# A gated long convolution on one core: fourth stage and projections in two column halves, sums and differences two tiles ahead, late taps in two pieces

## The chip, the cores and the metric

The kernel runs on one core of a Trainium2 chip. The metric is the device time of one execution in microseconds (us). The kernel before took 1112.37 us, the median of three runs that lie between 1107.36 and 1112.41 us. The profile is of one execution of its own, which took 1113.34 us; the span in the profile, from the first to the last instruction, is 1111.3 us.

In this text PE is the matrix engine and PEld its weight loads, DVE the vector engine, ACT the scalar engine, POOL the GpSimd engine, and SP the engine that issues the DMAs.

## The reference, cut to what matters

```python
def _attn_ref(x, h):                     # x: 8 x 6400 x 128, h: 6400 x 128, float32
    B, S, D = x.shape
    Xf, Hf = np.fft.rfft(x, n=2 * S, axis=1), np.fft.rfft(h, n=2 * S, axis=0)
    return np.fft.irfft(Xf * Hf[None], n=2 * S, axis=1)[:, :S, :]

def _moe_ref(x, w_val, conv_w, w_out):   # w_*: 128 x 128, conv_w: 5 x 128
    xp = np.concatenate([np.zeros((B, 4, D)), x], axis=1)
    gate_pre = sum(conv_w[k] * xp[:, k:k + S, :] for k in range(5))
    gate = 1.0 / (1.0 + np.exp(-gate_pre))
    return gate * (x @ w_val) @ w_out    # x is what _attn_ref returned
```

A causal convolution over 6400 steps for each of 128 channels and 8 batches, then a gate from five taps of its result, a projection, the product of both, and a second projection. All of it is float32.

## The kernel before, in words

**The transform.** The convolution is done by a real transform of length 6400 = 100 x 64, in stages that are matrix products. A time step t is 64 * n1 + n2. *Stage one* (`Forward`) folds the first 50 values of n1 onto the last 50: it needs the sum and the difference of two halves of a tile of x, and multiplies each with a constant `r1_sb`. *Stage two* (`s2_mm`) transforms over the 64 values of n2 with the matrices `m2`, of which four blocks are held at a time; `Product` multiplies its result with the spectrum of h (`h_sb`, kept in DRAM as `hd`). *Stage three* (`s3_quads`) is the inverse over 64, and *stage four* (`Chunk.s4`) the inverse over 100, with constants `m4_sb`. Stage four leaves channels on the partitions, and chunks of five n2 with 100 times each; `CHUNKS` has twelve of them and a first one of four (`HEAD`).

**Each chunk** then goes through `copies` (ACT: start the tap sums, copy the chunk `y`, scale one tap into `p`), `taps` (DVE: three multiply-adds of 500 columns; POOL: the fourth tap from `p`), `project` (PE: with `w_val`), `sigm` (ACT), `gate` (DVE), `output` (PE: with `w_out`) and `store` (ACT copy, then a DMA).

**The order** is written by hand and kept (`_Engines`, lines 88 to 105): each engine's queue runs in the order of the program text, so a wait of its front instruction holds all behind it. All instructions are recorded on line 96, which is that helper's; groups are told apart by the tiles they write and read (`pt` is any PSUM tile, `m_sb` stands for `m4_sb` and for the parts of it that hold input tiles in the startup, `r_sb` for both constants).

- *Startup*: stage one for h and for x of batch 0 (16 halves of a tile each; an input tile `x_sb` holds 8 channels of both halves and serves two calls of `half`), then stage two of both in turn, `Spectrum` and `Product`, for 13 blocks `kb`.
- *For each batch b*, stage three in 16 steps g, and beside it, half by half, stage one of the next batch (lines 570 to 584). `sums`, every second g, gives POOL the difference into `d_sb` and DVE the sum in place into the x tile; the matrix products of that tile come right behind, in the same step. The last chunks of the batch before are finished beside it, one item of `trail` a step. In batch 0, which has no such items, the loads of `m4_sb` and 22 small DVE operations that decode the weights (`weights`, one `next` each) stand there instead.
- Then stage four in 13 steps s, and beside it stage two of the next batch with its products (lines 592 to 625). A step gives PE: stage two of block s + 1, `project` of chunk s - 2, stage four of chunk s, `output` of chunk s - 3. It gives DVE: `mul_u` (named `gy<-pt,h` in the profile) and `mul_t` (`w<-pt,h`) of block s, with `taps` of chunk s - 1 between them, then `gate` of chunk s - 2. POOL adds the product terms (`gy<-gy,w`).
- Chunks from `DEFER` on (50 and 55) are *late*: only `y` is copied in stage four, and their taps (four on DVE, read from SBUF), gate and store are items of `trail`.

PSUM has two tiles of two banks for stages one and two and four single banks for the rest (in the startup four tiles of two banks).

Of the kernel before, what the change touches and what calls it, by code (L numbers as in the profile page):

```python
# [15 lines left out]
C = 128  # L16
# [8 lines left out]
XG = 8  # L25
NS = C // (2 * XG)
NQ = 2 * NS
NW = 2 * C + TAPS
CH = 5
# [5 lines left out]
DEFER = 50  # L35
# [3 lines left out]
XB = 2  # L39
# [69 lines left out]
def longconv_moe(ctx: ExitStack, tc: tile.TileContext, x, h, r1, m2, r3, m4, w64, out):  # L109
# [24 lines left out]
    d_sb = [cp.tile([128, XG, N2], F32, name=f"d_{i}") for i in range(2)]  # L134
# [74 lines left out]
    class Forward:  # L209


        def __init__(self, src, dst, xs=x_sb):
            self.src, self.dst, self.xs, self.n, self.i = src, dst, xs, 0, 0
# [7 lines left out]
        def sums(self):  # L221
            j = self.i // 2
            x, d = self.xs[j % len(self.xs)], d_sb[j % 2]
            nc.gpsimd.tensor_tensor(out=d, in0=x[:, 0], in1=x[:, 1], op=ALU.subtract)
            nc.vector.tensor_tensor(out=x[:, 0], in0=x[:, 0], in1=x[:, 1], op=ADD)

        def half(self):
            j, q = self.i // 2, self.i % 2
            self.i += 1
            x, d = self.xs[j % len(self.xs)], d_sb[j % 2]  # L230
            pt = pair()
            for m in range(4):
# [9 lines left out]
            if q:  # L242
                self.load()
            v = pt[:, :, : 4 * N1].rearrange("p r (d t k) -> p r d k t", t=2, k=N1)
            d0 = 4 * j + 2 * q
            return [
                lambda e, r=r: e(self.dst[:, r * C // 4 + d0 : r * C // 4 + d0 + 2], v[:, r]) for r in range(2)
            ]
# [109 lines left out]
    class Chunk:  # L358
# [8 lines left out]
        def s4(self):  # L367
            a, n = self.ch
            pt = single()
            for q in range(n):  # L370
                for c in range(2):
                    nc.tensor.matmul(
                        pt[:, q * N1 : (q + 1) * N1],
                        lhsT=dv[:, a + q, c, :],
                        rhs=m4v(a + q, c),
                        start=c == 0,
                        stop=c == 1,
                    )
            self.p = pt[:, : n * N1].rearrange("p (n t) -> p n t", n=n)
# [34 lines left out]
        def taps(self):  # L414
            a, n = self.ch
            if self.late:
                self.init()
# [8 lines left out]
            if k < n:  # L426
# [10 lines left out]
        def project(self):  # L437
# [3 lines left out]
            nc.tensor.matmul(self.v, lhsT=w_sb[:, :C], rhs=self.y, start=True, stop=True)  # L441
# [9 lines left out]
        def output(self):  # L451
# [3 lines left out]
            for i, o in cells(*self.ch):  # L455
                nc.tensor.matmul(self.o[:, i : i + o.shape[1]], lhsT=w_sb[:, C : 2 * C], rhs=o, start=True, stop=True)
# [13 lines left out]
        for i in range(6)  # L470
    ]
    fh, fx = Forward(h, gh, xh), Forward(x[0], gy, xh)
    nc.sync.dma_start(r1_sb, r1)
    fh.load(NS)
    for f in (fh, fx):
        for g in range(NQ):
            if g % 2 == 0:
                f.sums()
            e = f.half()
            if f is fh and g % 2:  # L480
                fx.load()
            e[0](act)
            e[1](act if g % 2 else dve)
        if f is fh:
            next(wgen)
# [4 lines left out]
    for kb in range(-1, NKB + 1):  # L490
# [8 lines left out]
        if 0 <= kb < NKB:  # L499
            pr[kb].mul_u()  # L500
# [6 lines left out]
    class Gates:  # L507
# [5 lines left out]
        def trail(self):  # L513

            h, i, j, k = (self.cs[i] for i in (0, NCH - 3, NCH - 2, NCH - 1))
            before = self.cs[NCH - 4]
# [20 lines left out]
        def each(self, what, s, last=True):  # L537
            c = self.at(s, last)
            if c:
# [10 lines left out]

    def m4_load(a, k):
        k = N2 + 1 if k == N2 else k
        nc.sync.dma_start(m4_sb[:, a:k], m4.rearrange("k (n t) -> k n t", t=N1)[:, a:k])
# [5 lines left out]
    for b in range(B):  # L559
# [26 lines left out]
        for _ in wgen:  # L586
            pass
# [86 lines left out]
```

## Time and profile before

| what | us |
|---|---|
| median of three runs | 1112.37 |
| the profiled execution | 1113.34 |
| its span | 1111.3 |
| startup, stage one of h and x (8.3 to 63.2) | 54.9 |
| startup, stage two of both (63.2 to 120.7) | 57.5 |
| stage three of batch 0, with stage one of batch 1 | 59.3 |
| stage three of batches 1 to 6, with stage one of the next, mean | 53.2 |
| stage four of batches 0 to 6, with stage two of the next, each | 73.3 |
| stage three of batch 7, nothing beside it | 39.7 |
| stage four of batch 7, nothing beside it, to the end | 59.1 |

The stages were told apart by the first matrix product of each kind: the stages three of batches 0 to 7 begin at 120.7, 253.3, 379.8, 507.0, 632.6, 758.8, 886.2 and 1012.5 us, the stages four at 180.0, 306.5, 433.7, 559.2, 685.4, 812.9, 939.2 and 1052.3 us. A float32 product is two instructions of the profile (two passes), each with its weight load. In a row of the timeline, the first number is the start and the second the length in us; the ends of pipelined matrix products are modelled, so the pace of a run of them is read from one start to the next.

### The profile page before, as it was taken

The numbers are of one execution on the slowest core, as the hardware profiler recorded it, in microseconds if no ns is written. First come the engines' busy times: TensorE is split into PE (matmuls) and PEld (weight loads), VectorE is DVE, ScalarE is ACT, GpSimd is POOL, SyncE is SP. The second block draws the span as 40 slices with busy tenths as digits, with TensorE's granted clock in tenths as the row PEclk, the third lists the DMA queues.
The fourth block names the chain that finished last, engine by engine and source line by source line (L and its number), as shares of the span: only waits on it lengthen the run. The fifth ranks groups of instructions, "written<-read, shape, count | busy, mean of one in ns | idle before, by whom it ended". The sixth has DMA issues, their size and how long they took to land.

```text
span 1111.3 us, 48967 instructions
## 1 busy us (share of the span) xinstructions
PE 1037.6 (93%) x22480; PEld 880.6 (79%) x22480; DVE 757.9 (68%) x1070; ACT 441.2 (40%) x825; POOL 447.1 (40%) x388
## 2 busy tenths in 40 slices
PE   6898779999999999999999999998999999999997
PEld 5798678877887778877898778877798778876875
DVE  2345656886588766987578765987578765986375
ACT  3332232543334443344434433343334443344365
POOL 3335412662156511753246511763136611753022
PEclk9999999999999999999999999999999999999999
DMA  6447634746266542756356552766346452751012
GB/s 246 153 142 234 253 126 144 229 135 223 84 193 187 186 149 89 234 158 216 96 176 187 163 181 86 226 162 231 96 151 198 128 212 69 240 157 50 20 34 85
DMA packets 86909, 175.80 MB, mean 158 GB/s; under 512 B 42288, under 2 KB 50736, under 8 KB 86704
## 3 DMA queue, kind: packets, MB, share of 16 engines
q1 hardware_dynamic: 86704, 172.68, 49.4%
q8 instruction: 176, 2.88, 1.1%
q14 instruction: 29, 0.24, 0.1%
HBM read 139.88 MB, written 32.77 MB: 155 GB/s over the span
## 4 chain that ended last, share of the span: by engine, by line
PE 86%; DVE 4%; issue 4%; DMA 2%; ACT 2%; POOL 1%; POOLq 0%; SPq 0%; DVEq 0%; ACTq 0%
PE pt L96 86%; DVE gl L96 2%; DMA x<-xl 2%; DVE dt L96 1%; DVE x L96 1%; POOL d L96 1%; ACT dt L96 1%; ACT gl L96 0%; DMA x<-hl 0%; ACT yl L96 0%; ACT gy L96 0%; POOL gy L96 0%; POOL dt L96 0%; DVE gy L96 0%; POOLq L670 0%
## 5 line engine op out<-in xcount | busy, mean ns | idle before, releaser
L96 PE MATMUL pt<-r_sb,gy 64*64 64x128 f32 (+1 forms) x8192 | 268.8, 273 | 26.2 <-issue 20.2
L96 PEld LDWEIGHTS pt<-r_sb,gy 64*64 64x64 f32 (+1 forms) x8192 | 236.6, 130 | 67.1 <-issue 40.0
L96 POOL TENSOR_TENSOR gy<-gy,w 128x512 f32<-128x512 f32 (+1 forms) x206 | 250.9, 1243 | 75.5 <-DVE w L96 74.7
L96 PEld LDWEIGHTS pt<-m_sb,dt 128*128 128x128 f32 x2048 | 242.8, 192 | 42.9 <-issue 35.8
L96 ACT COPY dt<-pt 128x512 f32<-128x512 f32 (+3 forms) x270 | 157.0, 585 | 248.2 <-PE pt L96 238.4
L96 PE MATMUL pt<-m_sb,dt 128*128 128x100 f32 x2048 | 244.9, 275 | 3.7 <-DVE dt L96 3.7
L96 PEld LDWEIGHTS pt<-gy,m 128*64 128x64 f32 x6400 | 197.1, 136 | 37.7 <-PE pt L96 28.9
L96 PE MATMUL pt<-gy,m 128*64 128x64 f32 x6400 | 209.4, 222 | 2.2 <-PE pt L96 2.1
L96 POOL TENSOR_TENSOR d<-x 128x512 f32<-128x512 f32 x60 | 76.4, 1279 | 273.4 <-DMA x<-xl 165.9
L96 DVE COPY dt<-pt 128x512 f32<-128x512 f32 (+1 forms) x136 | 92.9, 683 | 106.1 <-PE pt L96 87.1
L96 DVE SCALAR_TENSOR_TENSOR dt<-pt,w_sb,dt 128x500 f32<-128x500 f32 (+7 forms) x216 | 132.9, 631 | 39.5 <-ACT p L96 21.6
L96 PE MATMUL pt<-r_sb,d 50*64 50x100 f32 x2304 | 153.3, 277 | 1.3 <-issue 1.3
L96 PE MATMUL pt<-r_sb,x 50*64 50x100 f32 x1920 | 118.8, 258 | 23.3 <-DVE x L96 14.8
L96 PEld LDWEIGHTS pt<-r_sb,d 50*64 50x64 f32 x2304 | 132.9, 154 | 3.4 <-issue 3.4
L96 DVE COPY gy<-pt 128x400 f32<-128x400 f32 x120 | 68.9, 574 | 88.9 <-ACT gy L96 88.9
L96 DVE TENSOR_TENSOR gy<-pt,h 128x1024 f32<-128x1024 f32 (+1 forms) x98 | 115.0, 1173 | 19.3 <-PE pt L96 19.3
L96 PEld LDWEIGHTS pt<-r_sb,x 50*64 50x64 f32 x1920 | 102.7, 140 | 32.0 <-DVE x L96 18.7
L96 ACT ACTIVATE dt<-pt,w_sb 128x500 f32<-128x500 f32 (+1 forms) x64 | 40.0, 626 | 202.2 <-PE pt L96 202.2
L96 PE MATMUL pt<-dt,w_sb 128*128 128x500 f32 (+2 forms) x240 | 118.4, 583 | 0.4 <-ACT dt L96 0.4
L96 DVE TENSOR_TENSOR w<-pt,h 128x1024 f32<-128x1024 f32 (+1 forms) x98 | 114.8, 1171 | 0.0
L96 POOL TENSOR_TENSOR dt<-dt,p 128x500 f32<-128x500 f32 (+1 forms) x64 | 66.2, 1034 | 110.0 <-DVE dt L96 101.4
L96 DVE SCALAR_TENSOR_TENSOR gl<-pt,w_sb,gl 128x500 f32<-128x500 f32 (+3 forms) x119 | 74.1, 623 | 47.2 <-ACT gl L96 21.8
(38 smaller groups left out, 831.0 us busy)
## 6 DMA issues: line engine op xcount, KB each, us to landing
m<-m SPq DMA_DIRECT2D x96, 512.0 KB, 5.0
h<-hd SPq DMA_DIRECT2D x84, 512.0 KB, 4.8
x<-xl SPq DMA_DIRECT2D x58, 512.0 KB, 3.8
out<-dt SPq DMA_DIRECT2D x56, 250.0 KB, 4.1
out<-yl SPq DMA_DIRECT2D x40, 250.0 KB, 2.5
m_sb<-hl SPq DMA_DIRECT2D x6, 512.0 KB, 7.6
m_sb<-xl SPq DMA_DIRECT2D x6, 512.0 KB, 3.5
hd<-h SPq DMA_DIRECT2D x6, 512.0 KB, 5.4
```

The costliest lines, as they stand in the source:

```text
L96: return self._tc.keep_in_program_order(call(*args, **kwargs))
```

## The change

Seven edits, in the order of the diff:

1. A tile of x has 4 channels instead of 8 (`XG`), and one call of `half` uses it up; three input tiles instead of two, and three tiles `sd_sb` that hold sum and difference, instead of sums in place and two `d_sb`.
2. `sums` is called two tiles ahead of `half`. In the loop over batches both operations go to POOL; in the startup the sum stays on DVE. The next input load is issued by `sums`.
3. Stage four, `project` and `output` give PE two products of 64 columns of the weights where there was one of 128, into the two halves of the PSUM partitions.
4. Both results of stage one are taken out of PSUM by ACT in the loop over batches (before: one by ACT, one by DVE).
5. Chunk 45 becomes late too (`DEFER`), and the taps of the late chunks are issued in two pieces of two taps, in separate items of `trail`.
6. The loads of `m4_sb` and the decoding of the weights move from stage three of batch 0 into the startup's stage two.
7. The first load of h goes ahead of that of `r1`.

```diff
-XG = 8
+XG = 4
...
-DEFER = 50
+DEFER = 45
...
-XB = 2
+XB = 3
...
-    d_sb = [cp.tile([128, XG, N2], F32, name=f"d_{i}") for i in range(2)]
+    sd_sb = [cp.tile([128, 2, XG, N2], F32, name=f"sd_{i}") for i in range(3)]
...
-        def sums(self):
-            j = self.i // 2
-            x, d = self.xs[j % len(self.xs)], d_sb[j % 2]
-            nc.gpsimd.tensor_tensor(out=d, in0=x[:, 0], in1=x[:, 1], op=ALU.subtract)
-            nc.vector.tensor_tensor(out=x[:, 0], in0=x[:, 0], in1=x[:, 1], op=ADD)
+        def sums(self, e):
+            j = self.s
+            if j >= NS:
+                return
+            self.s += 1
+            x, sd = self.xs[j % len(self.xs)], sd_sb[(j + self.o) % 3]
+            nc.gpsimd.tensor_tensor(out=sd[:, 1], in0=x[:, 0], in1=x[:, 1], op=ALU.subtract)
+            e.tensor_tensor(out=sd[:, 0], in0=x[:, 0], in1=x[:, 1], op=ADD)
+            self.load()
...
-                        lhsT=(d if c else x[:, 0])[rows, 4 * q + m, :],
+                        lhsT=sd[rows, c, m, :],
...
-                    nc.tensor.matmul(
-                        pt[:, q * N1 : (q + 1) * N1],
-                        lhsT=dv[:, a + q, c, :],
-                        rhs=m4v(a + q, c),
-                        start=c == 0,
-                        stop=c == 1,
-                    )
+                    for k in range(2):
+                        o = slice(k * HP, (k + 1) * HP)
+                        nc.tensor.matmul(
+                            pt[o, q * N1 : (q + 1) * N1],
+                            lhsT=dv[:, a + q, c, o],
+                            rhs=m4v(a + q, c),
+                            start=c == 0,
+                            stop=c == 1,
+                        )
...
-            for j in range(4 if self.late else 3):
-                for i, o in cells(a + j, n):
-                    self.more(j, o, self.p[:, i : i + o.shape[1]])
+            for j in js:
+                if j < 3 or self.late:
+                    for i, o in cells(a + j, n):
+                        self.more(j, o, self.p[:, i : i + o.shape[1]])
...
-            nc.tensor.matmul(self.v, lhsT=w_sb[:, :C], rhs=self.y, start=True, stop=True)
+            for k in range(2):
+                o = slice(k * HP, (k + 1) * HP)
+                nc.tensor.matmul(self.v[o], lhsT=w_sb[:, o], rhs=self.y, start=True, stop=True)
...
-    nc.sync.dma_start(r1_sb, r1)
-    fh.load(NS)
-    for f in (fh, fx):
-        for g in range(NQ):
-            if g % 2 == 0:
-                f.sums()
-            e = f.half()
-            if f is fh and g % 2:
-                fx.load()
-            e[0](act)
-            e[1](act if g % 2 else dve)
...
+    fh.load()
+    nc.sync.dma_start(r1_sb, r1)
+    fh.load(len(xh) - 1)
+    order = [(f, i) for f in (fh, fx) for i in range(NS)]
+    for f, _ in order[:2]:
+        f.sums(nc.vector)
+    for g, (f, i) in enumerate(order):
+        e = f.half()
+        if g + 2 < 2 * NS:
+            order[g + 2][0].sums(nc.vector)
+        if g + len(xh) >= NS:
+            fx.load()
+        e[0](act)
+        e[1](act if g % 2 else dve)
...
         if 0 <= kb < NKB:
+            nc.sync.dma_start(
+                m4_sb[:, CH * kb : CH * kb + CH], m4.rearrange("k (n t) -> k n t", t=N1)[:, CH * kb : CH * kb + CH]
+            )
+        if 0 <= kb < NKB:
             pr[kb].mul_u()
             pr[kb].mul_t()
             pr[kb].add(nc.vector if kb == NKB - 1 else nc.gpsimd)
+            next(wgen, None)
+            next(wgen, None)
...
-                    (i.output, before.store),
-                    (i.store, j.taps),
-                    (j.project, j.sigm, j.gate),
-                    (j.output, k.taps),
-                    (j.store,),
-                    (k.project, k.sigm, k.gate),
-                    (k.output,),
-                    (k.store, h.project, h.sigm, h.gate),
-                    (h.output,),
+                    (z.store, lambda: i.taps(A)),
+                    (lambda: i.taps(Z),),
+                    (i.project, i.sigm, i.gate, lambda: j.taps(A)),
+                    (i.output, lambda: j.taps(Z)),
+                    (i.store, j.project, j.sigm, j.gate),
+                    (lambda: k.taps(A), j.output),
+                    (lambda: k.taps(Z), j.store),
+                    (k.project, k.sigm, k.gate),
+                    (k.output, h.project, h.sigm, h.gate),
+                    (k.store, h.output),
                     (h.store,),
...
-        for g in range(NQ):
-            if nxt and g % 2 == 0:
-                fx.sums()
+            for _ in range(2):
+                fx.sums(nc.gpsimd)
+        for g in range(NS):
             e = s3_quads(4 * g)
-            f = fx.half() if nxt else []
+            f = []
+            if nxt:
+                f = fx.half()
+                fx.sums(nc.gpsimd)
             e[0](act)
             e[1](dve)
-            if nxt:
-                f[0](act)
-                f[1](dve)
+            for u in f:
+                u(act)
             if trail:
                 trail.pop(0)()
-            if b == 0:
-                m4_load(4 * g, 4 * g + 4)
-                next(wgen, None)
-                next(wgen, None)
```

`output` is cut in the same way as `project`. In `trail`, `h` is the chunk of four, z, i, j and k are the chunks 40, 45, 50 and 55, and `A` and `Z` are the first and the last two of a late chunk's four taps.

Two places show how the order moves. The first is PE in a middle step of stage four: `gy,m` is stage two, `dt,w_sb` a projection, `m_sb,dt` stage four, and the last numbers are the output's partitions and columns. Before:

```order
L96 MATMUL pt_2992<-dt,w_sb 128x500
L96 MATMUL pt_2994<-m_sb,dt 128x100 x10
L96 MATMUL pt_3005<-dt,w_sb 128x500
L96 MATMUL pt_3023<-gy,m_3_82 64x32x2 x32
L96 MATMUL pt_3057<-dt,w_sb 128x500
```

and now:

```order
L95 MATMUL pt_3192<-dt,w_sb 64x500 x2
L95 MATMUL pt_3195<-m_sb,dt 64x100 x20
L95 MATMUL pt_3216<-dt,w_sb 64x500 x2
L95 MATMUL pt_3235<-gy,m_0_79 64x32x2 x32
L95 MATMUL pt_3269<-dt,w_sb 64x500 x2
```

The order is the same; every product but those of stage two, which had 64 output partitions before, has become two with 64 output partitions each.

The second is DVE at the start of stage three of batch 1, from the last gate of stage four on: `dt<-pt` takes stage three out of PSUM, `gy<-pt` stage one, `x<-x` is the sum of a tile, `gl<-yl,w_sb,gl` the taps of a late chunk, `gl<-pt,gl` a gate. Before:

```order
L96 TENSOR_TENSOR gl<-pt_3395,gl 128x500
L96 TENSOR_TENSOR x_86<-x_86 128x512
L96 COPY dt<-pt_3433 128x128x4
L96 COPY gy<-pt_3466 128x400
L96 SCALAR_TENSOR_TENSOR gl<-yl_77,w_sb,gl 128x500 x4
L96 COPY dt<-pt_3495 128x128x4
L96 COPY gy<-pt_3528 128x400
L96 TENSOR_TENSOR gl<-pt_3550,gl 128x500
L96 TENSOR_TENSOR x_87<-x_87 128x512
```

and now:

```order
L95 TENSOR_TENSOR w_92<-pt_3544,h_83 128x512
L95 SCALAR_TENSOR_TENSOR gl<-yl_76,w_sb,gl 128x500 x2
L95 COPY dt<-pt_3647 128x128x4
L95 SCALAR_TENSOR_TENSOR gl<-yl_76,w_sb,gl 128x500 x2
L95 COPY dt<-pt_3707 128x128x4
L95 TENSOR_TENSOR gl<-pt_3764,gl 128x500
L95 SCALAR_TENSOR_TENSOR gl<-yl_77,w_sb,gl 128x500 x2
L95 COPY dt<-pt_3773 128x128x4
```

The sums and the copies of stage one are gone from DVE's queue, no more than two taps stand between two copies of stage three, and a third chunk's taps and gate (`yl_76` is chunk 45) have come in from stage four.

More of the change, by code (lines that the diff above doesn't have):

```diff
@@ L209, in longconv_moe, with __init__ @@
     class Forward:
-        def __init__(self, src, dst, xs=x_sb):
-            self.src, self.dst, self.xs, self.n, self.i = src, dst, xs, 0, 0
+        def __init__(self, src, dst, xs=x_sb, o=0):
+            self.src, self.dst, self.n, self.s, self.i, self.o = src, dst, 0, 0, 0, o
+            self.xs = xs[o % len(xs) :] + xs[: o % len(xs)]
         def load(self, n=1):
@@ L219, in load @@
                     self.n += 1
-        def sums(self):
-            j = self.i // 2
-            x, d = self.xs[j % len(self.xs)], d_sb[j % 2]
-            nc.gpsimd.tensor_tensor(out=d, in0=x[:, 0], in1=x[:, 1], op=ALU.subtract)
-            nc.vector.tensor_tensor(out=x[:, 0], in0=x[:, 0], in1=x[:, 1], op=ADD)
+        def sums(self, e):
[7 more added lines that the diff above has]
+            self.load()
         def half(self):
-            j, q = self.i // 2, self.i % 2
+            j = self.i
             self.i += 1
-            x, d = self.xs[j % len(self.xs)], d_sb[j % 2]
+            sd = sd_sb[(j + self.o) % 3]
             pt = pair()
-            for m in range(4):
+            for m in range(XG):
                 for r, c in ((0, 0), (1, 1), (1, 0), (0, 1)):
@@ L241, in half @@
                     )
[L242 to L245, printed above, removed]
+            v = pt[:, :, : XG * N1].rearrange("p r (d t k) -> p r d k t", t=2, k=N1)
+            d0 = j * XG // 2
             return [
-                lambda e, r=r: e(self.dst[:, r * C // 4 + d0 : r * C // 4 + d0 + 2], v[:, r]) for r in range(2)
+                lambda e, r=r: e(self.dst[:, r * C // 4 + d0 : r * C // 4 + d0 + XG // 2], v[:, r]) for r in range(2)
             ]
@@ L412, in init, with taps @@
                 self.first(4, o, self.p[:, i : i + o.shape[1]])
-        def taps(self):
+        def taps(self, js=range(4)):
             a, n = self.ch
-            if self.late:
+            if self.late and 0 in js:
                 self.init()
@@ L425, in taps @@
             k = HEAD[0] - a - 4
-            if k < n:
+            if k < n and 0 in js:
                 for i, o in cells(HEAD[0], n - k):
                     self.more(4, o, self.p[:, k:])
-            for j in range(4 if self.late else 3):
-                for i, o in cells(a + j, n):
-                    self.more(j, o, self.p[:, i : i + o.shape[1]])
+            for j in js:
+                if j < 3 or self.late:
+                    for i, o in cells(a + j, n):
+                        self.more(j, o, self.p[:, i : i + o.shape[1]])
             if self.late:
@@ L455, in output @@
             for i, o in cells(*self.ch):
-                nc.tensor.matmul(self.o[:, i : i + o.shape[1]], lhsT=w_sb[:, C : 2 * C], rhs=o, start=True, stop=True)
+                for k in range(2):
+                    w = w_sb[:, C + k * HP : C + (k + 1) * HP]
+                    nc.tensor.matmul(
+                        self.o[k * HP : (k + 1) * HP, i : i + o.shape[1]], lhsT=w, rhs=o, start=True, stop=True
+                    )
         def store(self):
@@ L469, in longconv_moe @@
         )
-        for i in range(6)
+        for i in range(12)
     ]
-    fh, fx = Forward(h, gh, xh), Forward(x[0], gy, xh)
+    fh, fx = Forward(h, gh, xh), Forward(x[0], gy, xh, NS)
+    fh.load()
     nc.sync.dma_start(r1_sb, r1)
-    fh.load(NS)
-    for f in (fh, fx):
-        for g in range(NQ):
-            if g % 2 == 0:
-                f.sums()
-            e = f.half()
-            if f is fh and g % 2:
-                fx.load()
-            e[0](act)
-            e[1](act if g % 2 else dve)
-        if f is fh:
-            next(wgen)
+    fh.load(len(xh) - 1)
[10 more added lines that the diff above has]
+        e[1](act if g % 2 else dve)
+    next(wgen)
     for kb in range(M2B):
@@ L513, in trail @@
         def trail(self):
-            h, i, j, k = (self.cs[i] for i in (0, NCH - 3, NCH - 2, NCH - 1))
-            before = self.cs[NCH - 4]
+            h, z, i, j, k = (self.cs[i] for i in (0, NCH - 4, NCH - 3, NCH - 2, NCH - 1))
+            A, Z = range(2), range(2, 4)
             return [
@@ L538, in each @@
             c = self.at(s, last)
-            if c:
+            if c and not c.late:
                 getattr(c, what)()
@@ L549, in finish @@
             self.each("gate", s - 2)
-    def m4_load(a, k):
-        k = N2 + 1 if k == N2 else k
-        nc.sync.dma_start(m4_sb[:, a:k], m4.rearrange("k (n t) -> k n t", t=N1)[:, a:k])
     trail = []
```

4 lines of the change are left out of this document (1 added, 3 removed).

## The prediction

> **What bounds the kernel now.** First the page: busy times, and the chain of work that ended last.
>
> ```profile
> PE 1037.6 (93%) x22480; PEld 880.6 (79%) x22480; DVE 757.9 (68%) x1070; ACT 441.2 (40%) x825; POOL 447.1 (40%) x388
> PE 86%; DVE 4%; issue 4%; DMA 2%; ACT 2%; POOL 1%; POOLq 0%; SPq 0%; DVEq 0%; ACTq 0%
> ```
>
> PE is the bound nearly everywhere. So the question is in which stage PE works, in which it waits, and at what pace it works. Then the windows by stage (length, busy us and instructions of PE, PEld, DVE, ACT, POOL, PE clock, DMA share, GB/s):
>
> ```profile
> 8.30:63.20 54.90, 47.02 (x1026) 42.58 (x1026) 18.18 (x31) 21.18 (x46) 19.28 (x14) 1.00 0.46 161
> 63.20:120.70 57.50, 50.22 (x1604) 49.68 (x1601) 30.06 (x28) 13.63 (x15) 29.33 (x24) 0.97 0.66 213
> 120.70:180.00 59.30, 46.64 (x1537) 42.82 (x1537) 34.13 (x62) 16.78 (x31) 11.25 (x9) 0.94 0.50 175
> 180.00:253.30 73.30, 72.98 (x1099) 60.65 (x1098) 59.62 (x80) 31.59 (x58) 45.45 (x41) 1.00 0.60 173
> 253.30:306.50 53.20, 48.89 (x1550) 41.94 (x1549) 33.26 (x51) 21.27 (x41) 8.73 (x7) 1.00 0.45 155
> ```
>
> Stage four (the fourth row, seven times) has no idle PE at all: only a faster pace helps there. The other four have 4 to 13 us in which PE is not busy. Third, the timeline of one step of stage four:
>
> ```profile
> 329.85 2.37 PE L96 MATMUL pt<-m_sb,dt 128*128 128x100 f32 x20
> 331.01 1.22 DVE L96 TENSOR_TENSOR w<-pt,h 128x1024 f32<-128x1024 f32 x1
> 332.06 1.06 PE L96 MATMUL pt<-dt,w_sb 128*128 128x400 f32 x4
> 332.14 0.67 DVE L96 TENSOR_TENSOR dt<-pt,dt 128x500 f32<-128x500 f32 x1
> 332.73 1.22 DVE L96 TENSOR_TENSOR gy<-pt,h 128x1024 f32<-128x1024 f32 x1
> 333.05 2.09 PE L96 MATMUL pt<-gy,m 128*64 128x64 f32 x64
> 334.07 2.29 DVE L96 SCALAR_TENSOR_TENSOR dt<-pt,w_sb,dt 128x500 f32<-128x500 f32 x3
> 335.07 1.10 PE L96 MATMUL pt<-dt,w_sb 128*128 128x500 f32 x2
> 336.01 0.36 PE L96 MATMUL pt<-m_sb,dt 128*128 128x100 f32 x2
> ```
>
> From 329.85 to the next stage four at 336.01 a step takes 6.16 us (6.12 to 6.16 in its neighbours): stage four 2.21 (20 passes, 110 ns each), a projection 0.99, stage two 2.02 (64 passes, 31.6 ns each, or 63 ns for a pair of column halves), a projection 0.94.
>
> **Term A: stage four in halves, -57 us.** What a pair of halves costs at 100 columns no row shows for 128 rows. The nearest rows are stage two above (63 ns a pair at 64 columns) and stage one, which has 100 columns in four quarters of the array:
>
> ```profile
> 253.33 1.98 PE L96 MATMUL pt<-r_sb,gy 64*64 64x128 f32 x64
> 255.13 0.25 PE L96 MATMUL pt<-r_sb,x 50*64 50x100 f32 x1
> 255.30 0.24 PE L96 MATMUL pt<-r_sb,x 50*64 50x100 f32 x1
> 255.82 2.06 PE L96 MATMUL pt<-r_sb,gy 64*64 64x128 f32 x61
> ```
>
> The two middle rows are the first products of a group of four and of the next but one: a group starts every 86 ns, 0.86 ns a column. Stage four at 110 ns for the same 100 columns is thus not held by the columns that stream. The bounds for a pair are 63 ns (stage two) and 98 ns (stage two's 63 scaled from 64 to 100 columns, if the two streams shared a port). I take 87, by stage one, the nearest in columns. A chunk then costs 20 x 87 ns = 1.74, 0.47 less. A projection's two passes of 500 columns cost 0.86 by the same 0.86 ns, together 0.2 less. The step becomes 5.47 (from 6.13).
>
> DVE comes next. From start to start its step is 1.13 (`w`), 0.59 (gate), 1.14 (`gy`) and 2.3 (taps), so 5.16; the durations in the rows overlap and add up to 5.40. Both lie just under 5.47, so PE keeps the step, with DVE nearly full. In the early steps DVE holds it already:
>
> ```profile
> 316.85 1.23 DVE L96 TENSOR_TENSOR gy<-pt,h 128x1024 f32<-128x1024 f32 x1 [0.17 <-PE pt L96]
> 317.99 2.40 DVE L96 SCALAR_TENSOR_TENSOR dt<-pt,w_sb,dt 128x400 f32<-128x400 f32 x6
> ```
>
> It hardly pauses there (the bracket is the idle time before a row), so I count 0.6 for steps 0 to 3, 7 x 0.66 = 4.6 for steps 4 to 10, and 1.1 for the last two, which have two chunks and a short stage two. Two projections of chunk 45 (some 1.8) move to stage three. That is 8.1 off each of seven stages: 57 us.
>
> **Term B: stage three of batches 1 to 6, -19 us.** Now PE waits for sums that stand in DVE's queue behind taps, gates and copies:
>
> ```profile
> 257.72 3.07 DVE L96 SCALAR_TENSOR_TENSOR gl<-yl,w_sb,gl 128x500 f32<-128x500 f32 x4 [0.51 <-ACT gl L96]
> 263.11 0.30 PE L96 MATMUL pt<-r_sb,x 50*64 50x100 f32 x1 [1.48 <-DVE x L96]
> L96 PE MATMUL pt<-r_sb,x 50*64 50x100 f32 x1920 | 118.8, 258 | 23.3 <-DVE x L96 14.8
> ```
>
> With sums two tiles ahead on POOL these waits go, those of DVE's copies behind four taps too. PE's work is 16 x (1.80 from 253.33 to 255.13, and 0.69 from there to 255.82) = 39.8; eight projections (six before) at some 1.1 with the gaps around them, 8.8; 0.4 for the last copy. That is 49.0. What is late next is PE's own issue: 1 us for that, so 50 against 53.2, six times. POOL's two operations a step (0.73 each, below) stand beside a step of 2.5, on an engine busy 8.73 of 53.2 us, with two tiles of lead; ACT's 16 further copies (at most the 0.57 that they take on DVE, below) beside 21.27. If that cover went, a step would wait some 0.5 to 0.7. In SP's queue each load now waits for the two sums ahead of it, and stores of the late chunks wait behind it; nothing waits for those stores inside the stage.
>
> **Term C: stage three of batch 0, -15 us.** PE's two groups of products of stage three, between 126.5 and 180 us, then the second of them between 283 and 306 (batch 2), and a DMA queue of the page (packets, MB, share):
>
> ```profile
> L96 PE MATMUL pt<-r_sb,gy 64*64 64x128 f32 x480 | 28.6, 278 | 7.2 <-issue 7.2
> L96 PE MATMUL pt<-r_sb,gy 64*50 64x128 f32 x480 | 28.3, 274 | 2.0 <-issue 2.0
> ...
> L96 PE MATMUL pt<-r_sb,gy 64*50 64x128 f32 x256 | 14.9, 270 | 1.3 <-issue 1.2
> ...
> q8 instruction: 176, 2.88, 1.1%
> ```
>
> So 9.2 us of idle time are PE's own issue, which had nothing to wait for that the profile shows, against 1.2 in the later stretch. I take it that PE's instructions come late (the page's q8 loads instructions by DMA) while data are moved densely. The 3.3 MB of `m4_sb` leave this stage, the weight operations too, and 39.8 + 0.4 + 4 (between 1.2 and 9.2) gives some 44.3 against 59.3. The bounds are 41 and 50.
>
> **Term D: startup, stage one, -20 us.** Two halves take 3.46 us there, from copy to copy, and PE's wait is for the sum behind the copy:
>
> ```profile
> 13.98 0.57 DVE L96 COPY dt<-pt 128x400 f32<-128x400 f32 x1 [2.26 <-ACT dt L96]
> 14.47 0.68 DVE L96 TENSOR_TENSOR m_sb<-m_sb 128x512 f32<-128x512 f32 x1
> 17.44 0.57 DVE L96 COPY dt<-pt 128x400 f32<-128x400 f32 x1 [2.29 <-ACT dt L96]
> ...
> 8.57 0.37 PE L96 MATMUL pt<-r_sb,x 50*64 50x100 f32 x1
> 8.73 0.37 PE L96 MATMUL pt<-r_sb,x 50*64 50x100 f32 x1
> ...
> L96 PE MATMUL pt<-r_sb,x 50*64 50x100 f32 x128 | 11.7, 372 | 9.9 <-DVE x L96 8.8 <-issue 1.0
> ```
>
> A group starts every 0.16 us, at half the pace of stage three, and the mean of 372 ns over the whole stretch says that this lasts, whatever its clock column shows. 16 x 2.65 of work and 16 x 0.81 of wait make the 55 us. Without the waits at the slow pace: 42.4. With PE at the pace of stage three, POOL's difference and DVE's sum behind it set it; half tiles are priced by
>
> ```profile
> L96 POOL TENSOR_TENSOR gy<-gy,w 128x256 f32<-128x256 f32 x14 | 9.9, 728 | 0.0
> ```
>
> DVE's sum of half a tile is half of the 0.68 above, and may have to wait until POOL is done (the row in term E is such a case). So a tile costs 0.73 + 0.35, some 1.1: five tiles at the slow 1.33, then 27 x 1.1, 36 in all. The first load is half as large, and the start moves from 8.3 to an estimated 6 to 7. I take the fast pace after five tiles, because the same products in stage three, where waits are rarer, have a mean of 258 ns (term B's third row): end at 43 instead of 63.2. The bounds: 48 (slow) and 40.
>
> [...]
>
> **Term E: startup, stage two, +4 us.** It gets 22 weight operations, two a block behind `mul_t`, just when POOL adds. In the stage they leave, such a pair took
>
> ```profile
> 135.04 1.53 DVE L96 TENSOR_SCALAR gl<-gl 128x261 int32<-128x261 int32 x2
> ...
> L96 DVE TENSOR_SCALAR gl<-gl 128x261 f32<-128x261 f32 x3 | 0.9, 290 | 0.0
> ```
>
> 1.53 beside POOL, where it is 0.29 an operation by the second row. DVE is idle for 27 of the 57.5 us, 2.1 a block, which hides most; I take 0.3 a block, 11 times, and 1 for `m4_sb`, which comes on top of the 213 GB/s. The bounds are 0 (all hidden) and +14 (0.95 lost in each of 11 blocks, and the 3.9 that stage three of batch 0 lost more in issue than I give it).
>
> **Term F: batch 7, -2.5 us.** Its stage three keeps its pace: without stage one beside it, eight projections instead of six cost what the shorter tap pieces save. Stage four gains little: taps (1088.92), POOL's add and the next taps are a ring of 2.29 + 1.25 and two hand-overs, some 3.8 of 3.91:
>
> ```profile
> 1088.92 2.29 DVE L96 SCALAR_TENSOR_TENSOR gl<-pt,w_sb,gl 128x500 f32<-128x500 f32 x3 [1.06 <-POOL gl L96]
> 1091.35 1.25 POOL L96 TENSOR_TENSOR gl<-gl,p 128x500 f32<-128x500 f32 x1 [2.69 <-DVE gl L96]
> ```
>
> **Sum:** -57 - 19 - 15 - 20 + 4 - 2.5 = -109.5 from the profiled execution's 1113.3 (span 1111.3 and 2.0 around it), which is 1 us above the median: 1003 us.
>
> **The rivals.**
>
> *Weight loads come out from under the products (slower).* If a half's load did not run under the other half's product, a pair would cost the stream and a load of 64 columns: 87 + 55 (half of stage four's 110) = 142 ns. Over the 2048 pairs of eight batches that is 113 more, and 432 passes of projections add some 16: 1133. It decides from 140 ns a pair (87 + 109.5 us / 2048). Against it stands stage two: its pairs start every 63 ns, which leaves no room for load and product in turn. [...] Chance 0.04.
>
> *The halves share a stream:* 98 ns a pair, 0.49 a projection pass: 5.1 more a stage, seven times, 1040. Stage three's pace (1.80 for 16 groups of 128 columns, 0.88 ns a column in four quarters) speaks against it. Chance 0.07.
>
> *DVE becomes the bound in stage four:* it waits for ACT's `p` before the taps; if 0.5 us of waits a step stay, the step is 5.9, 0.45 x 7 x 7 = 22: 1025. For it: DVE at 95%. Against it: it has work of other chunks before each wait. Chance 0.17.
>
> *The change doesn't do what it says in stage three:* the waits for sums go, and issue gaps take their place: B nothing, C -9: 1028. Chance 0.15.
>
> *Issue gaps go everywhere,* C at 41, B at 49, and DVE keeps pace in the early steps: 985. Chance 0.07.
>
> **How the numbers follow.** The forecast, 990 to 1015, has 0.50; the startup at the slow pace is in it. The bounds of C, D and E add some 15 us on either side. 982 to 1045 takes in all but the slower rival and pairs of bad cases. A measurement of this kernel can tell 0.5% (5.6 us) from no change: faster 0.95, within it 0.01, slower 0.04.
>
> **What would show it.** Passes of stage four start every 43 to 44 ns, a middle step takes 5.5 and PE has no idle time there; a step of 5.9 with DVE waiting for `p` is the third rival, a pair over 100 ns the first or second. Stage three of batches 1 to 6 shows no wait of PE for a sum and takes 50. The startup's stage one shows means near 250 ns and ends by 43. I am wrong by most if the pair's pace is.

## The result, and the profile after

The changed kernel takes 1051.3 us, the median of four runs between 1048.06 and 1056.66, against 1112.4 for the kernel before beside it: a ratio of 0.946 (95% interval 0.9407 to 0.9512). The forecast of 1003 us had the sign right and the size wrong; the time lies 6 us above the range. The profiled execution took 1050.98 us.

By stages, from the first product of one to the first of the next (us):

| stage | term | before | after | difference | forecast |
|---|---|---|---|---|---|
| startup, stage one (to its end) | D | 63.2 | 45.2 | -18.0 | -20 |
| startup, stage two | E | 57.5 | 65.6 | +8.1 | +4 |
| stage three of batch 0 | C | 59.3 | 54.4 | -4.9 | -15 |
| stage three of batches 1 to 6, sum | B | 319.3 | 344.1 | **+24.8** | -19 |
| stage four of batches 0 to 6, sum | A | 513.3 | 443.7 | -69.6 | -57 |
| batch 7, both stages | F | 98.8 | 95.9 | -2.8 | -2.5 |

So one row, 44 us off its forecast, is nearly as large as the whole miss of 48 us: stage three of batches 1 to 6 became longer where it was to become shorter. The misses of the other rows nearly cancel: C, D and E together gave 16 us less than forecast, A 13 more. The page of the changed kernel, busy times and the chain that ended last:

```profile
PE 959.7 (92%) x24960; PEld 804.9 (77%) x24960; DVE 681.7 (65%) x925; ACT 481.1 (46%) x930; POOL 541.4 (52%) x565
PE 82%; DMA 6%; issue 5%; DVE 4%; POOL 2%; SPq 1%; ACT 1%; POOLq 0%; DVEq 0%; ACTq 0%
```

PE is still the bound, but DMA has gone from 2% of the chain to 6%. That points at the loads, but it is not their price, since the chain leaves out what PE did meanwhile. The windows by stage (columns as before: length, busy times of PE, PEld, DVE, ACT, POOL, PE clock, DMA share, GB/s), for the startup's two stages, stages three and four of batch 0, and stage three of batches 1 and 2:

```profile
3.90:45.20 41.30, 33.23 (x1024) 30.25 (x1024) 26.09 (x47) 20.60 (x46) 25.55 (x32) 0.92 0.71 256
45.20:110.80 65.60, 50.89 (x1604) 49.61 (x1600) 46.23 (x51) 13.63 (x15) 30.43 (x24) 0.97 0.70 232
110.80:165.20 54.40, 47.62 (x1537) 45.17 (x1538) 12.36 (x17) 22.71 (x46) 23.65 (x33) 0.88 0.41 137
165.20:228.40 63.20, 61.59 (x1390) 51.58 (x1388) 55.73 (x74) 29.82 (x55) 43.81 (x40) 1.00 0.69 198
228.40:283.10 54.70, 49.49 (x1572) 41.32 (x1570) 24.83 (x33) 28.48 (x58) 23.45 (x31) 1.00 0.47 155
346.50:403.90 57.40, 52.32 (x1570) 43.56 (x1568) 24.34 (x33) 28.57 (x58) 23.33 (x31) 0.94 0.45 149
```

No engine is full in stage three (POOL, which took over the sums, is busy 23 of 57 us), and PE stands for 5 us in each. The timeline of PE in the first steps of batch 2 (start, duration, what, in brackets the idle time before and its cause):

```profile
355.48 0.87 PE L95 MATMUL pt<-r_sb,gy 64*64 64x128 f32 x24 [1.59 <-issue]
...
358.18 1.98 PE L95 MATMUL pt<-r_sb,gy 64*64 64x128 f32 x64
363.58 1.61 PE L95 MATMUL pt<-r_sb,sd 50*64 50x100 f32 x32 [3.42 <-POOL sd L95]
365.12 1.93 PE L95 MATMUL pt<-yl,w_sb 128*64 128x500 f32 x4
366.98 3.27 PE L95 MATMUL pt<-r_sb,gy 64*64 64x128 f32 x64
370.08 0.86 PE L95 MATMUL pt<-r_sb,sd 50*64 50x100 f32 x32
```

PE waits 3.42 us for POOL's sums of the fourth tile, and what follows the wait runs at half pace (granted clock 0.50 from 362.85 to 369.68, below): stage one 1.61 where it is 0.86 a step later, 64 products of stage three 3.27 where they took 1.98 in the step before. Counted from start to start, that is 2.9 us more. What POOL waited for, and what stood in SP's queue (same columns; two views of the same kernel):

```profile
346.41 4.37 POOL L95 TENSOR_TENSOR sd<-x 128x256 f32<-128x256 f32 x5
362.12 4.13 POOL L95 TENSOR_TENSOR sd<-x 128x256 f32<-128x256 f32 x6 [11.35 <-DMA x<-xl]
```

```profile
347.74 1.82 SPq L95 DMA_DIRECT2D m<-m  x4
349.67 1.77 SPq L95 DMA_DIRECT2D h<-hd  x3
351.53 15.08 SPq L95 DMA_DIRECT2D x<-xl  x6
```

POOL was done with the three tiles in stock at 351 and then stood for 11.35 us, until the fourth tile landed. That tile's load was issued at 351.53, behind seven loads for the coming stage four. Over batches 1 to 6 PE waits 22.3 us for POOL's sums, 3.1 to 4.2 in each. In 40 slices of 346 to 370 us (0.6 us each) the GB/s moved were:

```profile
GB/s 137 0 0 147 321 150 232 184 376 396 423 430 376 389 403 430 410 430 403 417 416 420 372 376 242 82 58 41 27 0 24 174 253 68 283 92 201 362 310 95
```

The seven loads are 512 KB each, 3.67 MB in all (the expectations below say 3.3, which was too low); at 400 GB/s that is 9 us. The kernel before had the same seven loads ahead at the same place:

```profile
253.63 2.55 SPq L96 DMA_DIRECT2D m<-m  x4
256.28 1.61 SPq L96 DMA_DIRECT2D h<-hd  x3
...
258.71 9.33 SPq L96 DMA_DIRECT2D x<-xl  x2
```

But its two tiles in stock held four steps' work, and a tile was summed in the step that used it. Three smaller tiles hold three steps' work, and are summed two steps ahead: the loads of the change come due earlier, behind the same 9 us.

### The profile page after: what moved, and what is told of

The parts are those of the page before. It is cut to its first block, busy times and chain, and to the rows that moved or that the text cites. A ratio compares the mean times of both kernels' runs of the same rounds, so it can differ in the third digit from the quotient of the medians.

```text
span 1048.9 us, 54153 instructions
## 1 busy us (share of the span) xinstructions
PE 959.7 (92%) x24960; PEld 804.9 (77%) x24960; DVE 681.7 (65%) x925; ACT 481.1 (46%) x930; POOL 541.4 (52%) x565
## 3 DMA queue, kind: packets, MB, share of 16 engines
q8 instruction: 196, 3.21, 1.3%
## 4 chain that ended last, share of the span: by engine, by line
PE 82%; DMA 6%; issue 5%; DVE 4%; POOL 2%; SPq 1%; ACT 1%; POOLq 0%; DVEq 0%; ACTq 0%
PE pt L95 82%; DMA x<-xl 6%; DVE gl L95 2%; DVE dt L95 1%; SPq L95 1%; POOL sd L95 1%; POOL gl L95 1%; DVE gy L95 0%; DVE sd L95 0%; POOL dt L95 0%; DVE w L95 0%; ACT dt L95 0%; DMA out<-yl 0%; DMA x<-hl 0%; ACT gy L95 0%
## 5 line engine op out<-in xcount | busy, mean ns | idle before, releaser
L95 POOL TENSOR_TENSOR sd<-x 128x256 f32<-128x256 f32 x232 | 174.5, 778 | 193.6 <-issue 85.9
L95 PEld LDWEIGHTS pt<-m_sb,dt 128*64 128x64 f32 x4096 | 190.8, 137 | 46.3 <-issue 34.4
L95 PE MATMUL pt<-m_sb,dt 128*64 128x100 f32 x4096 | 198.0, 250 | 2.9 <-DVE dt L95 2.4
L95 PE MATMUL pt<-r_sb,sd 50*64 50x100 f32 x4608 | 148.3, 262 | 43.1 <-POOL sd L95 22.3
L95 PEld LDWEIGHTS pt<-r_sb,sd 50*64 50x64 f32 x4608 | 131.6, 143 | 52.2 <-POOL sd L95 24.4
L95 ACT COPY gy<-pt 128x400 f32<-128x400 f32 x248 | 110.1, 496 | 74.9 <-PE pt L95 68.6
L95 PE MATMUL pt<-dt,w_sb 128*64 128x500 f32 (+2 forms) x480 | 115.2, 559 | 0.7 <-DVE dt L95 0.4
L95 DVE SCALAR_TENSOR_TENSOR gl<-yl,w_sb,gl 128x500 f32<-128x500 f32 (+1 forms) x91 | 79.0, 869 | 35.8 <-ACT gl L95 34.3
L95 DVE SCALAR_TENSOR_TENSOR gl<-pt,w_sb,gl 128x500 f32<-128x500 f32 (+4 forms) x98 | 58.6, 598 | 32.9 <-ACT gl L95 27.5
L95 ACT COPY yl<-pt 128x500 f32<-128x500 f32 (+1 forms) x96 | 54.2, 565 | 47.8 <-PE pt L95 47.8
```

The lines of the kernel that those rows point to most:

```text
L95: return self._tc.keep_in_program_order(call(*args, **kwargs))
```

## The experiments

All times are beside the kernel before on the same chip (1109 to 1115 us); the changed kernel's is 1051.3. Two theories on stage three were tried first: the load order (Q), and PE's own issue (I).

**e1: sums, and the loads that they release, ahead of the seven loads.**

```diff
         if nxt:
+            for _ in range(2):
+                fx.sums(nc.gpsimd)
             for kb in range(M2B):
                 m2_load(kb)
             for kb in range(HB):
                 h_load(kb)
-            for _ in range(2):
-                fx.sums(nc.gpsimd)
```

> The changed kernel, with the two sums at the start of each stage three (and the loads of the fourth and fifth tile that they release) put ahead of the seven loads for the next stages (four of m, three of hd, 3.3 MB). Theory Q (the fourth tile is late because its load stands behind those seven): the wait for POOL's sum (3.4 to 5 us) and the half pace behind it go, stage three of batches 1 to 6 falls from 57.3 to 50 to 52, that of batch 0 from 54.4 to about 53, the whole to about 1013 to 1020 us. Rival P (POOL, with two sums a tile, cannot keep up): the same 57 and 1051, with POOL without idle time in the first steps. Rival I (PE's own issue, slowed by dense transfers, takes what the sums free): 55 and more, about 1038.

1022.96 us, ratio 0.9177 (0.9128 to 0.9225), 3 us above the expectation of Q; the startup in its profile is 2.8 us longer than that of the changed kernel, with the same code. Stage three of batches 1 to 6 falls from 344.1 to 312.4 us (52.1 each), that of batch 0 from 54.4 to 51.7. SP's queue, stage three of batch 2 as a window, and the waits of PE in it (total, times, longest):

```profile
347.38 1.14 SPq L95 DMA_DIRECT2D x<-xl  x2
348.57 3.34 SPq L95 DMA_DIRECT2D m<-m  x4
352.01 1.76 SPq L95 DMA_DIRECT2D h<-hd  x3
```

```profile
346.20:398.40 52.20, 49.38 (x1570) 41.66 (x1568) 24.52 (x33) 28.67 (x58) 24.73 (x31) 1.00 0.50 163
```

```profile
PE pt L95 <- issue: 2.8, 3, 1.7
```

The wait for POOL is gone and, in this batch, so is the half pace (clock 1.00). Theory Q holds and P falls: POOL does the same 31 operations in 24.73 us, where they took 23.33. It is 32 of B's 44 us: the 22.3 of the waits, and for the most part the half pace behind them. What PE still waits for is its own issue, 1.3 to 3.3 us a stage (all idle time of PE counted; the view leaves out stops under 0.15).

**e2: as e1, with the seven loads one a step, in steps 0 to 6.**

```diff
                 fx.sums(nc.gpsimd)
+                if g < M2B:
+                    m2_load(g)
+                elif g < M2B + HB:
+                    h_load(g - M2B)
```

> As the run before, and the seven loads one a step, in steps 0 to 6 of stage three. Theory Q: as the run before, 1013 to 1020. Theory I (dense transfers delay PE's instructions): the issue gap of 1.6 to 1.9 us in the third step goes as well, stage three of batches 1 to 6 reaches 49 to 50 and batch 0 about 50, the whole 1000 to 1008. If neither holds, 1051 as the changed kernel.

1022.52 us (0.9173), stage three 52.1: the same as e1. The gaps are as long (1.0 to 4.7 a stage), only elsewhere. That the gaps are there because of dense transfers is not refuted by it (e9 below), but that spreading them is enough is.

**e4 and e5: the halves alone, and all but the halves.** e4 is the kernel before with the new `s4`, `project` and `output`; e5 the changed kernel with the old ones:

```diff
                 for c in range(2):
-                    nc.tensor.matmul(pt[:, q * N1 : (q + 1) * N1], lhsT=dv[:, a + q, c, :], rhs=m4v(a + q, c), ...)
+                    for k in range(2):
+                        o = slice(k * HP, (k + 1) * HP)
+                        nc.tensor.matmul(pt[o, q * N1 : (q + 1) * N1], lhsT=dv[:, a + q, c, o], rhs=m4v(a + q, c), ...)
```

> The kernel before, with nothing of the change but stage four and the projections in two halves. Theory H (the gain of the change is the halves' alone): stage four falls from 73.3 to 63 to 65.5 (two projections and a chunk's taps more than in the changed kernel), stage three stays at 53, the whole 1050 to 1056 us. Rival D (DVE's order or the two projections moved into stage three made a part of the 10 us): stage four 68 or more, the whole over 1075.

> The changed kernel with stage four and projections in full width again. Theory H: stage four rises from 63.3 to 71 to 73, stage three keeps its 55 to 59 (the projections in it 0.15 longer each), the whole 1108 to 1116 us, about the kernel before: the other edits together are worth nothing. Rival (the other edits gain some 15 to 20 us in the startup and lose them nowhere): 1095 or less.

e4 takes 1062.01 us (0.9527, 0.9484 to 0.957), e5 1118.59 (1.0038, 1.0018 to 1.0059). One stage four of e4, and one of e5, as windows:

```profile
301.20:366.30 65.10, 63.52 (x1398) 54.15 (x1396) 59.21 (x79) 30.17 (x57) 44.14 (x39) 1.00 0.70 196
```

```profile
296.50:368.00 71.50, 71.16 (x1094) 59.82 (x1094) 56.13 (x74) 28.26 (x54) 45.38 (x42) 1.00 0.60 174
```

Over the seven stages the halves take 8.0 us off each (65.3), the two projections moved out of it 1.7 (71.6), and both together 9.9. H holds: without the halves, the other edits make the kernel 0.4% slower; with them, they take 1062 to 1051. e4 came out 6 us above the end of its expectation, since its startup (125.4 us against 120.7) and stage three of batches 1 to 6 (54.3 against 53.2) were longer than in the profile of the kernel before.

**e6, e7, e8: the startup's stage two.** On top of e1: in e6 the weight operations go back to stage three of batch 0; in e7 the loads of `m4_sb` go to stage three and stage four of batch 0, five rows from each end at a time; in e8 both. The first two lines of the diff stand in stage three (e6), the next two there, and the last two in stage four (e7); what stood in the startup's loop is taken out there.

```diff
+            if b == 0 and g > 1:
+                next(wgen, None); next(wgen, None)
+            if b == 0 and g in (8, 11):
+                m4_rows(g // 11)
...
+            if b == 0 and s < 5:
+                m4_rows(s + 2)
```

> The kernel of e1 with the 22 weight operations taken out of the startup's stage two and put into stage three of batch 0, two a step from its third step on, as the kernel before had them (one earlier step there). Theory W (DVE, held by POOL in these operations, is what makes the startup's stage two longer, 65.6 us in the changed kernel against 57.5): that stage falls to 59 to 62, the whole by 4 to 6 from e1's 1023. Theory M (the loads of m4 are, by way of PE's instructions that come late): the stage keeps 64 to 67, the whole is within 3 of e1, since DVE has idle time for the operations in either place.

> The kernel of e1 with the loads of m4_sb taken out of the startup's stage two: the rows of the first two chunks are loaded in stage three of batch 0, those of the other chunks in its stage four, three chunks ahead. Theory M: the issue gaps of PE in the startup's stage two, 12.7 us in the changed kernel, fall to about 5 (before: 4 to 5), the stage to 57 to 59, the whole to 1014 to 1018; stage four of batch 0, which issues 42 instructions a us and not 77, keeps 63 to 65. Theory W: the stage keeps 64 to 67 and the whole stays within 3 of e1's 1023.

> Both edits of e6 and e7 on top of e1. If M alone holds, the same as e7 (1014 to 1018); if both cost, 1010 to 1013; if what limits the stage is a third thing, 1020 and more.

1031.4, 1024.99 and 1024.13 us (e8 0.9244, 0.9188 to 0.93; its four runs lie between 1014.64 and 1029.3). PE's waits in that stage, in this order:

```profile
PE pt L95 <- issue: 13.9, 9, 2.3
```

```profile
PE pt L95 <- issue: 11.8, 10, 1.7
```

```profile
PE pt L95 <- issue: 2.4, 2, 2.3
```

The stage is 68.2, 65.4 and 55.3 long. Neither W nor M holds alone, and one short stage in e8's profile (its fastest run) did not make its median shorter. Of e6's 8 us above e1, 7 stand in stage three of batches 1 to 6 (319.8 us against 312.4), which the edit doesn't touch, so single profiles of the same code can differ by that much. The stage also varies with the code unchanged: 57.5 and 63.6 in the profiles of the kernel before and of e4, 64.0 to 69.7 in seven profiles with the startup of the changed kernel, and 55.3 and 61.5 in those of e8 and e11, which have the same startup.

**e9: as e1, without the seven loads in stage three of batches 1 to 6.**

```diff
-            for kb in range(M2B):
-                m2_load(kb)
-            for kb in range(HB):
-                h_load(kb)
+            if b == 0:
+                for kb in range(M2B):
+                    m2_load(kb)
+                for kb in range(HB):
+                    h_load(kb)
```

> The kernel of e1 without the seven loads at the start of stage three in batches 1 to 6 (their first blocks of stage two then use stale m and hd). Theory I (PE's instructions come late because dense transfers hold them up): the issue gaps of these stages, 1.3 to 3.3 us in e1 (mean 2.3), fall under 1, the stages from 52.1 to 50 or less. Rival R (the round trip of the instruction load itself limits a stage that issues 77 instructions a us, with or without other transfers): gaps of 1.3 to 3.3 stay, the stages 51 to 53.

1009.67 us in one run. The stages take 48.7 to 51.0 us, 49.6 in the mean, with gaps of 0 to 1.8 (0.6). That of batch 1 has none at all:

```profile
231.70:280.40 48.70, 48.69 (x1572) 41.32 (x1570) 25.62 (x33) 28.59 (x58) 24.57 (x31) 1.00 0.32 99
```

Their sum, 297.6 us, lies well below that of every other version with e1's or a later order (312.4 to 319.8), so one run is enough here: most of the gaps (0.6 us a stage here, 2.3 in e1) are there because other data move, and I holds for the cause.

**e12: as e1, with 4.5 MB less to load in the startup's stage two.** The nine later loads of m are left out (the last is half as large; the expectation has 4.6).

```diff
             pr[kb] = Product(kb, sp[kb].h)
-            m2_load(kb + M2B)
```

> The kernel of e1 without the nine later loads of m in the startup's stage two (its blocks 4 to 12 use stale data; 4.6 MB less beside it). Theory I: PE's issue gaps there (11 to 14 us in five profiles of this code) fall under 4, the stage from 65.5 to 69.5 down to 55 to 58. Rival (the gaps come from the load of instructions by itself, whatever else moves): they keep 10 or more.

One run, 1015.17 us. The stage falls to 57.6 us. PE's waits in it, in the changed kernel and in e12:

```profile
PE pt L95 <- issue: 11.0, 8, 2.2
```

```profile
PE pt L95 <- issue: 4.2, 7, 1.1
```

That is about the size expected of the same cause, but one run doesn't show it for this stage: e7, with 3.3 MB less to load and the same 184 GB/s as e12, kept 11.8 us of gaps, and the kernel before and e8 had 3.9 and 2.4 beside 213 and 217 GB/s. How much is moved does not decide alone.

**e10, e11, e13: three tries to win e9's time without leaving the loads out.** e10 issues the seven loads at the end of the stage four ahead, each as its buffer comes free; e11 adds e8 to it; e13 is e2 with the loads in every second step (`if g % 2`, with `g // 2` for `g`). The diff is e10's, in stage four, with e9's behind it:

```diff
                 m2_load(s + 1 + M2B)
+                if b + 2 < B and s + 1 >= NKB - M2B:
+                    m2_load((s + 1) % M2B)
...
                 h_load(s + HB)
+                if b + 2 < B and s >= NKB - HB:
+                    h_load(s % HB)
```

> The kernel of e1, with the seven loads of stage three of batches 1 to 6 moved to the end of the stage four ahead of it, each as soon as its buffer is free. Theory I (dense transfers delay PE's instructions only where PE issues 77 a us): stage three falls to 49 to 50.5 as in e9 (49.6), stage four stays at 63.3 to 64.5, the whole about 1008 (1004 to 1012). Rival (the transfers only move their cost): stage four 65 and more, the whole within 4 of e1's 1023.

> e10 and both edits of e8 (m4_sb and the weight operations out of the startup's stage two). The startup's stage two was 55.3 in the profile of e8, but its other runs were 7 to 15 us longer: 995 to 1000 where it is the short one, else as e10 (1004 to 1012).

> The kernel of e2 with the seven loads one in every second step of stage three (steps 1, 3, ... 13) in place of one in each of steps 0 to 6. Theory I, where what counts is how much else moves when an instruction load is due: gaps between e9's 0.6 and e2's 2.4 us a stage, stage three of batches 1 to 6 50 to 51.5 (52.1 in e1 and in e2), the whole 1012 to 1018. If it is enough that one 512 KB load meets it, the gaps keep 2 to 3 us and the whole 1020 to 1026.

1021.14 (0.9172, 0.9126 to 0.9219), 1023.87 (0.9215) and 1030.21 us (0.9263, 0.9224 to 0.9302): none beats e1. In e10 stage four did not grow (63.6 us), so the rival's time came without its reason. The last of the seven and the loads of x meet at the border, and its stage three is 50.6 in batch 1 and 57.2 in batch 4. In e13 the gaps are those of the second alternative (2.5 us a stage), though 1030 us lies above its range as well: of the 8.8 us between the profiles of e13 and e1, 3.6 stand in the startup, which the edit doesn't touch. In batch 3 two 512 KB loads and one of x were issued at 503 to 505, and the longer of PE's two stops in that stage, 3.21 us, began at 508.62. SP's queue, then PE's:

```profile
503.14 0.83 SPq L95 DMA_DIRECT2D x<-xl  x1
504.02 0.90 SPq L95 DMA_DIRECT2D h<-hd  x2
```

```profile
507.25 1.37 PE L95 MATMUL pt<-r_sb,gy 64*64 64x128 f32 x43
511.83 1.30 PE L95 MATMUL pt<-r_sb,gy 64*50 64x128 f32 x17 [3.21 <-issue]
...
514.48 3.40 PE L95 MATMUL pt<-r_sb,gy 64*64 64x128 f32 x57
```

With a projection in a step PE issues more slowly (200 instructions in 3.6 us, against 192 in 2.5 without one), which may give it a reserve; the wide spread put the last loads into the steps without one, and the gap of 3.21 us there was followed by half pace (57 products in 3.40 us at 514.48, 53 in 1.69 at 518.53). That the reserve is the reason is argued, not shown. So e1, with 1023 us, is the version that beats both kernels, e2 and e10 being no different from it.

## Why the prediction was wrong, step by step

**What bounds the kernel:** right. PE's work in stage three, 49.0 us by the sum, is what e9 shows (48.7).

**Term B, wrong in sign; here the prediction failed.** The step is the sentence on what covers POOL's work: its sums "with two tiles of lead", and "in SP's queue each load now waits for the two sums ahead of it". It followed each load back to the sums, and did not look at what stands ahead of it in the same queue. The lead was counted in tiles of sums, where the lead that runs out is that of tiles in stock: three steps, some 12 us from the start of the stage, against a load that landed 15.6 us after it. No rival had this case. Of the 44 us, e1 gives back 32. The other 12 are PE's issue: 1 us a stage was forecast, 2.3 came (e1), and a stop costs some more behind it where half pace follows (2.9 us behind the 3.42 above). With the order mended the kernel stands at 1023, near what the fourth rival gave (issue gaps take the place of the waits, 1028), but not for that rival's reason. By the waits view the gaps of these six stages sum to 15.4 us in the kernel before and to 13.2 in e1: they did not take the waits' place, they were there already, and the sum, which read one batch, took them too small.

**Term A, right in mechanism, too small.** A step of the changed kernel, the timeline of PE and of DVE:

```profile
420.51 1.02 PE L95 MATMUL pt<-dt,w_sb 128*64 128x500 f32 x4
421.35 1.90 PE L95 MATMUL pt<-m_sb,dt 128*64 128x100 f32 x40
423.13 2.10 PE L95 MATMUL pt<-gy,m 128*64 128x64 f32 x64
425.05 1.02 PE L95 MATMUL pt<-dt,w_sb 128*64 128x500 f32 x4
```

```profile
425.10 2.29 DVE L95 SCALAR_TENSOR_TENSOR dt<-pt,w_sb,dt 128x500 f32<-128x500 f32 x3 [0.29 <-issue]
427.30 1.22 DVE L95 TENSOR_TENSOR w<-pt,h 128x1024 f32<-128x1024 f32 x1
```

From start to start the rows are 0.84, 1.78 and 1.92 (later 1.72, which is 43.0 ns a pass, and 1.87), and a middle step takes 5.27. The pair of halves is the 87 ns of the forecast (86). Stage two, which the sum took over unchanged at its old 2.02, fell to 1.87; a projection takes 0.84, with 0.86 counted. DVE kept pace, with 0.29 us idle here; the third rival (DVE becomes the bound) did not come. At 86 ns a pair, with 142 for weight loads that come out and 98 for a shared stream, the first two rivals did not come either.

**Term C, a third of the forecast.** The issue gaps fell from 10.2 us (9.2 in the forecast's rows) to 6.2, where 4 were counted, and half pace cost some 7 (clock 0.88 over the stage), for which the sum has no term. It came in two stretches of 6.83 us, one behind a gap of 2.92 us, the other behind a wait of 3.75 us for DVE just ahead of the stage. In e1 and the runs built on it this stage stays between 51.6 and 54.1. It has no projections, so PE issues at its highest rate (192 instructions in 2.5 us) in all 16 steps; that this is why is not shown.

**Term D, right in size, in part by luck:** it ends at 45.2 (forecast 43). No run of the kernel before shows the five slow tiles of the sum, which were the author's estimate; here the products had a mean of 372 ns up to 11.28 us, in the fifth tile, and of 248 from 11.5 to 15.2. But the stage started earlier (3.9, not 6 to 7) and ran longer (41 us, not 36), two errors that nearly cancel: DVE's half sums took 690 ns beside POOL where 340 were counted, and issue gaps cost 5.4 us.

**Term E, within its bounds, for the other reason.** DVE's operations were to cost most; e6 took them away and the stage kept 68.2. The time went into issue gaps, 11.0 us against 3.9. Since the code of the kernel before gave 57.5 and 63.6, a part of the 8 us is chance; why either edit alone, e6 or e7, keeps the long gaps stays open. (The 3.9 in this term's upper bound should be 5.2, that is 9.2 less 4; the bound is then 16.)

**Term F, right:** 2.8 against 2.5.

## What to carry to other kernels

A lead counted in buffers has to be held against the time that its refill takes to land (here some 12 us of stock, and a load that landed 15.6 us after the start of the stage): follow a load back through its whole queue, with the bytes ahead of it, before a smaller tile or a shorter stock is called hidden. When prefetches for a later stage share a queue with loads that are due in a few steps, issue the loads that are due first (e1: 1023 us against 1051). And before waits are taken away in a stage with many small matrix products, count its instructions a us: here PE's own issue was what came late next in stage three, at 77 (13.2 us of gaps in six stages of e1), and in stage four, at 42, the changed kernel had no issue gap over 0.15 us.

## What the runs showed of the hardware

**PE's instructions came late in blocks.** In the trace of the changed kernel, all 21 issue gaps of PE over 0.6 us stand 256 instructions (products, weight loads and PE's semaphore waits together) or a multiple of that apart, give or take one, and each ends 1.3 to 1.7 us after a packet of the queue q8 (instructions, 16 KB) has landed. Four of stage two in the startup, from its records (us):

```
gap            instruction   packet of the block    end of gap - landing
74.98-77.23    3777          74.85-75.81            1.42
81.15-83.17    4033          80.66-81.74            1.43
87.14-88.56    4289          86.16-87.12            1.45
92.46-94.46    4545          92.17-93.05            1.41
```

From the end of one gap to the start of the next block's packet it took 3.0 to 3.6 us here; later in the same stage, from 94.46 on, 1.5 to 2.2. Stage three with stage one beside it issues 192 instructions in 2.5 us, a block in 3.3; stage four 224 in 5.27, a block in 6.0, and has no issue gap over 0.15 us. In stage three, at 77 instructions a us, the trace has five issue gaps of more than 1 us (at 121.66, 236.43, 353.88, 633.14 and 720.58); in the 3.3 us before them 400, 403, 385, 146 and 418 GB/s were moved. Its other six over 0.6 us are shorter than 1 us and came beside as little as 5 GB/s (768.7) and as much as 410 (841.1), so how much else moves does not decide alone here either.

**Half pace after a stop depended on where it fell.** The stop of 3.42 us above was followed by half pace; one of 3.59 us, at the same place in batch 1 of the same execution, was not:

```profile
244.99 0.92 PE L95 MATMUL pt<-r_sb,sd 50*64 50x100 f32 x32 [3.59 <-POOL sd L95]
245.84 1.06 PE L95 MATMUL pt<-yl,w_sb 128*64 128x500 f32 x4
```

In this execution's records of the granted clock, the half clock comes in stretches of 3.41 or 6.83 us that begin on a grid of 3.41 us. Cut along that grid, the two stops look so (columns as in the windows above; first batch 1, then batch 2):

```profile
239.97:243.38 3.41, 1.44 (x55) 1.18 (x44) 0.69 (x1) 0.58 (x1) 0.00 (x0) 1.00 0.81 305
243.38:246.80 3.42, 1.81 (x36) 0.92 (x36) 0.00 (x0) 0.82 (x3) 3.26 (x5) 1.00 0.22 47
359.44:362.85 3.41, 0.71 (x28) 0.46 (x20) 0.69 (x1) 0.59 (x1) 0.72 (x2) 1.00 0.51 184
362.85:369.68 6.83, 6.10 (x88) 4.29 (x92) 0.68 (x1) 1.88 (x4) 4.81 (x7) 0.50 0.51 157
```

The longer stop was shared by two windows, in which PE still worked 1.44 and 1.81 us, and the clock stayed full. The shorter one left a window with 0.71 us of work, and the clock was half from its end on. In this execution every window at the full clock with 2.0 us or more without PE's work was followed by the half clock, and of the others a single one, in the startup, so stops of 2.00, 2.45 and 2.92 us, with 2.0 us or more of them in one window, were enough too. The length of a stop alone did not decide in this execution: 3.59 us went without the half clock and 2.00 us with it.
